# Eighty stores of a convolution and attention kernel issued from ScalarE's queue instead of SyncE's

## The chip, the cores and the metric

The kernel runs on one core of a Trainium2 chip. A core has five engines that work at once, each through its own list of instructions in order: TensorE (PE in the profile, with its weight loads as PEld), VectorE (DVE), ScalarE (ACT), GpSimd (POOL) and SyncE (SP), which only waits and issues DMAs. They meet at semaphores. The metric is the device time in microseconds of one execution, as the median of several; shorter is better. Times inside an execution are read from its profile and count from the start of the span.

## What is computed

Two independent halves are concatenated along the last axis. `A` is a long convolution whose kernel comes from a diagonal state space, `B` is attention with a learned feature map and no softmax over positions. L = S = 2048, D = 576, 128 states, 32 heads of 18.

```python
def _A_ref(u, log_A_real, A_imag, C_real, C_imag, log_dt, D_skip):
    dt = jnp.exp(log_dt)
    A = -jnp.exp(log_A_real) + 1j * A_imag
    C = (C_real + 1j * C_imag) * dt[:, None]
    P = jnp.exp((A * dt[:, None])[:, :, None] * pos[None, None, :])
    K = 2.0 * jnp.einsum("dn,dnl->dl", C, P).real
    y = irfft(rfft(u_t, 2 * L) * rfft(K, 2 * L), 2 * L)[:, :, :L]
    return y.T + u * D_skip
def _B_ref(x, wqkv, w_phi, wo):
    q, k, v = heads of x @ wqkv
    phi_q = concat(softmax(q @ w_phi), softmax(-(q @ w_phi)))      # and phi_k from k
    num = phi_q @ (phi_k^T v);  den = phi_q @ sum(phi_k) + 1e-6
    return (num / den).reshape(B, S, D) @ wo
return jnp.concatenate([a, b], axis=-1)
```

## The kernel before, in words

Everything is one program of 2902 operations. `Plan` (L171 on in the file) collects them: `op(engine, cost, function, r=..., w=...)` notes which buffers an operation reads and writes. Nothing is scheduled when the kernel is built: the table `ORDER` lists the operations by number in the order in which `Plan.run` emits them, with the buffer slot that each new tile takes and, after a `+`, how many filler matmuls go ahead of it; a `*` takes an operation's second engine. Within the table each engine's instructions keep their order, so the table sets all five queues at once. The costs written beside the operations were for the making of the table; `run` does not look at them. A DMA is an operation of engine `"sp"` whose function calls `sp.dma_start`, so it is emitted at its place in the table and is issued by SyncE in that order. It waits on SyncE's queue until its tile has been written, and the DMAs behind it in the table wait with it.

`B` runs as 16 key tiles of 128 positions (`key_tile`), the state `kv`, and 16 query tiles (`query_tile`). A query tile multiplies by the folded weight `wqT`, makes two softmaxes (q1, q2), transposes the features into `fT` (q3), multiplies by `kvb` and divides into `o` (q4), transposes `o` into `x9` (q5), multiplies by `wo` (q6), copies two halves of 288 columns from PSUM into `ot` on ScalarE or VectorE, and stores `ot`, 128 rows of 2304 bytes, into the right half of the output (L739).

`A` is a Fourier transform in stages, with tensors in DRAM between them. `u_first` transforms the input into `ud` (store at L769). `params`, `phases`, `waves` and `group` make the convolution kernel, 36 groups in 18 pairs: `waves` runs `Abs` (L909) and four sines (L916, L917) on ScalarE; `group` runs three exponentials of a PSUM tile on ScalarE (L933, L940), products on VectorE and GpSimd (L944, L948, L950 and L462), and the 64 matmuls `ps<-E,cs`. `k_first` transforms the result into `kd` (store at L983). `product` does two halves of 288 channels times eight blocks: it loads the constants `ff`, two `ub` from `ud` (L1032) and two `kb` from `kd` (L1051), multiplies, and brings the result back in `zo`, two tiles that ScalarE or VectorE copies from PSUM; both are stored into `zd[half]` (L1097), 128 rows of two runs of 1152 bytes each. `last` runs sixteen times: it loads `zi` from `zd[half]` (L1107), multiplies, copies one PSUM tile into `yo` on ScalarE or VectorE, adds and subtracts on VectorE (L466), and stores `yo` in two halves of 64 rows into the left half of the output (L1122).

The stages are not one after the other: `ORDER` mixes operations of both halves on all engines. The three kinds of store named above, 16 at L739, 32 at L1097 and 32 at L1122, lie between 252.6 and 536.5 us of the span. The PSUM tiles `ps` are 8 in all; `zo`, `ot`, `yo`, `ub`, `kb`, `fT` and others share 19 slots of one pool. L452 is the copy helper (on ScalarE and on VectorE), L455 its ScalarE form with another output type, L447 the matmul helper, L462 and L466 the tensor-tensor helper; a line of the profile with one of these stands for many places, and the tile's name tells which.

Of the kernel before, what the change touches and what calls it, by code (L numbers as in the profile page):

```python
# [170 lines left out]
class Plan:  # L171
# [24 lines left out]
    def op(self, eng, cost, fn, r=(), w=(), with_=(), table=None, busy=1.0, lock=False, mode=(128, 128), add=None):  # L196
        deps = set()
        for b in r:
            deps.update(b.writers)
        for b in w:  # L200
            deps.update(b.readers)
        if eng == "pe":
            deps.update(self.zero.writers, self.data.writers)
        k = len(self.ops)
        eng, alt = eng if isinstance(eng, tuple) else (eng, None)
        cost, alt = cost if alt is None else cost[0], alt and (alt, cost[1])
        for b in r:
            b.readers.append(k)
        for b in w:
            b.writers.append(k)  # L210
        bufs = list({id(b): b for b in (*r, *w, *with_) if not isinstance(b, Mark)}.values())
        for b in bufs:
            b.left += 1
        fill = [b for b in w if b.tag == "ps" and b.writers == [k] and not b.readers] if eng == "pe" else []
        fill = [add] if add else fill
        self.ops.append([eng, cost, fn, deps, bufs, alt, table, busy, lock, (self.unit, self.part), mode, fill[0] if fill else None, add])
# [50 lines left out]
def c_dma(nbytes, run=4096):  # L267
    return nbytes / run * (0.35 + 0.0029 * run)
# [158 lines left out]
def body(tc, nc, i, out, ctx):  # L427
    pl = Plan()
    pe, dve, act, pool, sp = nc.tensor, nc.vector, nc.scalar, nc.gpsimd, nc.sync
# [14 lines left out]
    B, op = pl.buf, pl.op  # L444

    def mm(o, l, r, start=True, stop=True, skip=False):
        pe.matmul(o, l, r, start=start, stop=stop, skip_group_check=skip)  # L447
# [102 lines left out]
    def load_again(t):  # L550
        x9 = B("x9", [128, 9, 128], F32R)
        op("sp", c_dma(128 * 4608), lambda: sp.dma_start(flat9(x9), xd[t].t), r=[xd[t]], w=[x9])
        return x9
# [15 lines left out]
    def gemm_halves(x, w, done, c0):  # L569
        r = []  # L570
        for cs, need in zip(halves, done):
            ps = B("ps", [128, 288])
            gemm(x, w, need, ps, lambda ps=ps: ps.t, slice(c0 + cs.start, c0 + cs.stop))
            r.append(ps)
        return r
# [105 lines left out]
    def query_tile(t):  # L681
        pl.at("query", t)
        ps = gemm_halves(load_again(t), wqo, (have_q[0:3], have_q[2:5]), 0)
        pl.step("q1")
        e = softmax([(ps[c], slice(16 * c, 16 * c + 16), lambda c=c: ps[c].t.rearrange("p (h f) -> p h f", f=DH)) for c in range(2)], True)
        pl.step("q3")
        fT = []
        rows = lambda j: 18 * GRP[j // 2]

        def turn(j0, n):  # L690
            tp, m, f4 = B("ps", [126, 4, 128]), rows(j0), B("fT", [126, 4, 128])
            fT.append(f4)

            def f():
                for j in range(j0, j0 + n):
                    g, sign = divmod(j, 2)
                    pe.transpose(tp.t[0:m, j - j0, :], e.t[:, sign, 7 * g:7 * g + GRP[g], :].rearrange("p h f -> p (h f)"), ident.t)  # L697
            op("pe", 110 * n, f, r=[e, ident], w=[tp], with_=[f4], busy=0.5)
            copy("any", lambda: f4.t[0:m, 0:n, :], lambda: tp.t[0:m, 0:n], [tp], [f4], 128 * n)
        for j0, n in ((0, 4), (4, 4), (8, 2)):  # L700
            turn(j0, n)
        pl.step("q4")
        o = B("o", [128, H, DH])

        def divide(g0, g1, h0, n):
            pn, den = B("ps", [128, 21, 19]), B("small", [128, 21])

            def f():
                for g in range(g0, g1):
                    hs, m = slice(7 * g, 7 * g + GRP[g]), rows(2 * g)  # L710
                    for sign in range(2):
                        j = 2 * g + sign
                        mm(pn.t[:, hs.start - h0:hs.stop - h0], fT[j // 4].t[0:m, j % 4, :], kvb.t[0:m, sign, 0:GRP[g], g, :], sign == 0, sign == 1)
            op("pe", 448 * (g1 - g0), f, r=[*fT[g0 // 2:(2 * g1 - 1) // 4 + 1], kvb], w=[pn], busy=0.4)
            op("dve", 80 + 6.7 * n, lambda: dve.reciprocal(den.t[:, :n], pn.t[:, :n, 18]), r=[pn], w=[den])
            tt("dve", lambda: o.t[:, h0:h0 + n], lambda: pn.t[:, :n, 0:18], lambda: den.t[:, :n, None].to_broadcast([128, n, DH]),
               ALU.mult, [pn, den], [o], 18 * n)
        divide(0, 3, 0, 21)
        divide(3, 5, 21, 11)
        pl.step("q5")  # L720
        tp, tq = B("ps", [128, 4, 128]), B("ps", [128, 128])
        of = lambda c: o.t.rearrange("p h f -> p (h f)")[:, c:c + 128]

        def f():
            for k in range(4):
                pe.transpose(tp.t[:, k], of(128 * k), ident.t)  # L726
            pe.transpose(tq.t, of(448), ident.t)
        op("pe", 550, f, r=[o, ident], w=[tp, tq], busy=0.5)
        o9 = B("x9", [128, 9, 128], F32R)
        copy("act", lambda: o9.t[:, 0:4], lambda: tp.t, [tp], [o9], 512)  # L730
        tt("dve", lambda: o9.t[:, 5:9], lambda: tp.t, lambda: o9.t[:, 0:4].bitcast(F32), ALU.subtract, [tp, o9], [o9], 512)
        copy("act", lambda: o9.t[64:128, 4], lambda: tq.t[64:128], [tq], [o9], 260)
        tt("dve", lambda: o9.t[0:64, 4], lambda: tq.t[64:128], lambda: o9.t[64:128, 4].bitcast(F32), ALU.subtract, [tq, o9], [o9], 245)
        pl.step("q6")
        po = gemm_halves(o9, wqo, (have_o[0:2], have_o[1:3]), D)
        ot = B("ot", [128, D])
        for c, cs in enumerate(halves):
            copy("any", lambda c=c, cs=cs: ot.t[:, cs], lambda c=c: po[c].t, [po[c]], [ot], 288)
        op("sp", c_dma(128 * 2304, 2304), lambda: sp.dma_start(out[t * 128:t * 128 + 128, 576:1152], ot.t), r=[ot])  # L739

    for t in range(NT):
        query_tile(t)
# [3 lines left out]
    kd, zd = ([B("dram", [64, 64, HD]) for _ in range(2)] for _ in range(2))  # L746
# [249 lines left out]
    par = [None] * NB  # L996
# [21 lines left out]
    def product(p, half):  # L1018
# [11 lines left out]
        four = lambda z, par: z.t[32 * par + 4 * p:32 * par + 4 * p + 4].rearrange("(j r) s d -> (r s) j d", r=2)  # L1030
# [50 lines left out]
        pz, zo = [B("ps", [128, HD]) for _ in range(4)], [B("zo", [128, 2, HD]) for _ in range(2)]  # L1081
# [10 lines left out]
        for c in range(4):  # L1092
            j, par = divmod(c, 2)
            copy("any", lambda c=c, j=j, par=par: zo[par].t[:, j], lambda c=c: pz[c].t, [pz[c]], [zo[par]], HD)

        for par in range(2):
            op("sp", c_dma(128 * 2304, 1152), lambda par=par: sp.dma_start(four(zd[half], par), zo[par].t), r=[zo[par]], w=[zd[half]])  # L1097

    for half in range(2):
        for p in range(8):  # L1100
            product(p, half)


    def last(i0, half):
        pl.at("last", 8 * half + i0 // 2)
        yo, zi = B("yo", [128, 2, HD]), B("zi", [128, 2, 2, HD])
        op("sp", c_dma(128 * 4608, 2304), lambda: sp.dma_start(  # L1107
            zi.t, zd[half].t.rearrange("q (r z b) d -> (q r) z b d", r=2, z=2)[:, :, i0:i0 + 2]), r=[zd[half]], w=[zi])
        ps = [B("ps", [128, HD]) for _ in range(2)]
        pl.step("l1")  # L1110

        def f():
            for z in range(2):
                for n in range(2):
                    mm(ps[z].t[64 * n:64 * n + 64], w3.t[:, 64 * z:64 * z + 64], zi.t[:, z, n], True, True, True)
        op("pe", 970, f, r=[zi, w3], w=ps, with_=[yo], mode=(128, 64))
        copy("any", lambda: yo.t[:, 1], lambda: ps[1].t, [ps[1]], [yo], HD)
        for z, alu in enumerate((ALU.add, ALU.subtract)):
            tt("dve", lambda z=z: yo.t[:, z], lambda: ps[0].t, lambda: yo.t[:, 1], alu, [ps[0], yo], [yo], HD)
        for n in range(2):  # L1120
            st = out.ap[0][0]
            op("sp", c_dma(64 * 2304, 1152), lambda n=n: sp.dma_start(bass.AP(  # L1122
                tensor=out.tensor, offset=out.offset + (i0 + n) * st + HD * half, ap=[[32 * st, 64], [(31 - 2 * (i0 + n)) * st, 2], [1, HD]]),
                yo.t[64 * n:64 * n + 64]), r=[yo])

    for half in range(2):
        for i0 in range(0, 16, 2):
            last(i0, half)
# [22 lines left out]
```

## Time and profile before

| | |
|---|---|
| Median of 3 runs | 540.35 us (539.47 to 544.67) |
| Profiled execution: its own time, its span | 542.0 us, 540.2 us |
| Granted TensorE clock, mean | 0.987 |
| DMA packets, bytes | 77495, 116.41 MB |
| Mean DMA rate over the span | 215 GB/s |

The profile is of one execution. Its span runs from the first to the last instruction; its own time is 1.8 us longer than the span. Busy time of an engine is time in which an instruction of it was running; waiting, semaphore instructions and the issuing of DMAs do not count as busy. In a row of a view, `out<-in` are tiles by the program's names without buffer numbers, and `SPq` is SyncE's own queue.

### The profile page before, as it was taken

The numbers are of one execution on the slowest core, as the hardware profiler recorded it, in microseconds if no ns is written. First come the engines' busy times: TensorE is split into PE (matmuls) and PEld (weight loads), VectorE is DVE, ScalarE is ACT, GpSimd is POOL, SyncE is SP. The second block draws the span as 40 slices with busy tenths as digits, with TensorE's granted clock in tenths as the row PEclk, the third lists the DMA queues.
The fourth block names the chain that finished last, engine by engine and source line by source line (L and its number), as shares of the span: only waits on it lengthen the run. The fifth ranks groups of instructions, "written<-read, shape, count | busy, mean of one in ns | idle before, by whom it ended". The sixth has DMA issues, their size and how long they took to land.

```text
span 540.2 us, 19689 instructions
## 1 busy us (share of the span) xinstructions
PE 519.9 (96%) x8186; PEld 437.3 (81%) x8186; DVE 449.5 (83%) x994; ACT 413.8 (77%) x730; POOL 331.0 (61%) x375
## 2 busy tenths in 40 slices
PE   6899999999999988999999999999999999999996
PEld 5799998999988767798887767866788887767985
DVE  3799988999999986998988989997986769878463
ACT  2699998999869977989899689799687454564442
POOL 0376798988987975975675579678454354340400
PEclk8999999999999998999999999998999999999999
DMA  8697975923317695573487956696567777997786
GB/s 227 191 358 232 350 229 202 292 80 97 119 45 234 155 324 160 139 234 109 140 225 263 303 158 199 196 277 232 176 194 233 237 216 221 289 340 241 263 265 177
DMA packets 77495, 116.41 MB, mean 215 GB/s; under 512 B 9186, under 2 KB 54370, under 8 KB 77406
## 3 DMA queue, kind: packets, MB, share of 16 engines
q1 hardware_dynamic: 77406, 115.16, 67.9%
q8 instruction: 64, 1.05, 0.8%
q14 instruction: 25, 0.20, 0.1%
HBM read 65.87 MB, written 49.26 MB: 213 GB/s over the span
## 4 chain that ended last, share of the span: by engine, by line
PE 76%; ACT 10%; DVE 6%; DMA 3%; issue 3%; POOL 1%; SPq 0%; DVEq 0%; POOLq 0%; ACTq 0%
PE ps L447 71%; PE ps L697 3%; ACT ps L933 1%; PE ps L726 1%; DMA e<-in_wkT_dram 1%; ACT zi L452 1%; ACT cs L916 1%; ACT cs L917 1%; DMA ff<-in_ff_dram 1%; ACT e L592 1%; DVE cs L944 1%; DMA dram<-zi 1%; ACT cs L909 1%; DVE E L466 1%; DVE wl L514 1%
## 5 line engine op out<-in xcount | busy, mean ns | idle before, releaser
L447 PE MATMUL ps<-wh,x 128*128 128x288 f32 (+2 forms) x1008 | 241.3, 319 | 1.9 <-ACT wh L513 1.4
L447 PEld LDWEIGHTS ps<-wh,x 128*128 128x128 f32 x1008 | 174.3, 189 | 12.8 <-ACT wh L513 1.7
L447 PE MATMUL ps<-wl,x 128*128 128x288 f32 (+2 forms) x560 | 175.9, 315 | 0.4 <-DVE wl L514 0.4
L447 PEld LDWEIGHTS ps<-wl,x 128*128 128x128 f32 x560 | 106.1, 189 | 1.7 <-DVE wl L514 0.7
L899 POOL TENSOR_TENSOR cs<-cs,pi 128x64 int32<-128x64 int32 (+4 forms) x90 | 91.5, 1017 | 6.1
L462 POOL TENSOR_TENSOR E<-v,cs 128x512 f32<-128x512 f32 x30 | 38.5, 1303 | 32.7 <-ACT v L940 31.3
L595 POOL TENSOR_TENSOR o<-e 128x576 f32<-128x576 f32 x32 | 43.1, 1346 | 18.9 <-ACT e L592 16.3
L466 DVE TENSOR_TENSOR ac<-us,ps 128x576 f32<-128x576 f32 x64 | 45.2, 744 | 6.6 <-PE ps L447 5.8
L462 POOL TENSOR_TENSOR e<-e,small 128x576 f32<-128x576 f32 x30 | 36.2, 1208 | 19.6 <-DVE small L462 13.7
L944 DVE TENSOR_TENSOR cs<-ps,cs 128x1024 f32<-128x1024 f32 x36 | 43.7, 1215 | 4.8 <-ACT ps L933 4.7
L447 PEld LDWEIGHTS ps<-E,cs 128*32 128x32 f32 x2304 | 34.6, 110 | 14.3 <-issue 10.3
L447 PEld LDWEIGHTS ps<-kvb,fT 126*128 126x128 f32 (+1 forms) x320 | 39.7, 192 | 7.7 <-issue 1.8
L462 POOL TENSOR_TENSOR e<-small,e 128x576 f32<-128x576 f32 x29 | 34.0, 1172 | 19.4 <-DVE small L462 7.9
L933 ACT ACTIVATE ps<-ps 128x512 f32<-128x512 f32 x72 | 41.6, 588 | 4.4 <-PE ps L447 3.8
L447 PE MATMUL ps<-E,cs 128*32 128x64 f32 x2304 | 40.7, 221 | 4.1 <-issue 3.5
L592 ACT ACTIVATE e<-e 128x1152 f32<-128x1152 f32 x32 | 37.3, 1167 | 8.7 <-POOL e L462 8.7
L447 PE MATMUL ps<-kvb,fT 126*128 126x133 f32 (+1 forms) x320 | 42.9, 284 | 0.6 <-DVE ac L466 0.6
L447 PE MATMUL ps<-sel,mg 128*128 128x512 f32 x108 | 41.5, 443 | 1.4 <-DVE cs L944 0.6
L452 ACT ACTIVATE zi<-ps 128x288 f32<-128x288 f32 x95 | 33.6, 413 | 9.7 <-PE ps L447 9.3
L917 ACT ACTIVATE cs<-cs,hp 128x1024 f32<-128x1024 f32 x36 | 40.6, 1141 | 0.0
L909 ACT ACTIVATE cs<-cs 128x2048 f32<-128x2048 int32 x18 | 34.4, 1913 | 5.8 <-POOL cs L899 5.6
L916 ACT ACTIVATE cs<-cs 128x1024 f32<-128x1024 int32 x36 | 36.7, 1051 | 0.2
(145 smaller groups left out, 1047.4 us busy)
## 6 DMA issues: line engine op xcount, KB each, us to landing
xd<-x SPq DMA_DIRECT2D x16, 576.0 KB
dram<-zi SPq DMA_DIRECT2D x32, 288.0 KB
dram<-zi SPq DMA_DIRECT2D x16, 576.0 KB
x<-xd SPq DMA_DIRECT2D x16, 576.0 KB
kb<-dram SPq DMA_DIRECT2D x32, 288.0 KB
ub<-dram SPq DMA_DIRECT2D x32, 288.0 KB
dram<-zo SPq DMA_DIRECT2D x32, 288.0 KB
zi<-dram SPq DMA_DIRECT2D x16, 576.0 KB
```

Source lines behind the costliest of these rows:

```text
L447: pe.matmul(o, l, r, start=start, stop=stop, skip_group_check=skip)
L452: op(("act", "dve"), (c_act(n), c_dve(n)), lambda e: act.activation(dst(), src(), AF.Copy) if e == "act" else dve.tensor_copy(dst(), src() ...
L462: op(eng, [c_dve(n[0]) if e == "dve" else c_pool(n[1]) for e in eng], lambda e: (dve if e == "dve" else pool).tensor_tensor(dst(), a(), b( ...
L466: op(eng, c_dve(n) if eng == "dve" else c_pool(n), lambda: e.tensor_tensor(dst(), a(), b(), op=alu), r=r, w=w, with_=with_, lock=eng == "p ...
L592: op("act", c_act(1152) + 40, lambda: act.activation(e.t, e.t, AF.Exp), r=[e], w=[e], table="exp")
L595: op("pool", c_pool(517), lambda: pool.tensor_tensor(pair.t, e.t[:, :, :, 0:9], e.t[:, :, :, 9:18], op=ALU.add), r=[e], w=[pair], lock=True)
L899: op("pool", c_add(4 * n * W), lambda n=n, j=j: pool.tensor_tensor(x()[:, :, :, n:2 * n], x()[:, :, :, 0:n], pi.t[:, j:j + 2, gs].bitcast( ...
L909: op(("act", "dve"), (c_act(n) + 45, c_dve(n)), lambda e: act.activation(cs.t[:, 0], x(), AF.Abs) if e == "act" else dve.scalar_tensor_ten ...
L916: op("act", c_act(64 * W) + 150, lambda at=at: act.activation(at(1), at(1).bitcast(I32), AF.Sin, scale=TURN), r=[cs], w=[sine], with_=[cs] ...
L917: op("act", c_act(64 * W) + 225, lambda at=at: act.activation(at(0), at(0), AF.Sin, scale=-TURN, bias=hp.t), r=[cs, hp, sine], w=[both], w ...
L933: op("act", c_act(512) + 12, lambda: act.activation(ps.t, ps.t, AF.Exp), r=[ps], w=[ps], table="exp")
L944: op("dve", c_dve(64 * W), lambda: dve.tensor_tensor(F(), both(M.t), F(), op=ALU.mult), r=[M, ready], w=[long], with_=[cs])
```

## The change

The three stores call `act.dma_start` in place of `sp.dma_start`; `act` is `nc.scalar`, `sp` is `nc.sync`. Nothing else differs: the operations keep engine `"sp"` and their cost in the plan, and the order table is the same. The 80 DMAs stand at the same places in the table, and there they now belong to ScalarE's list of instructions, between the ScalarE operation that the table has before them and the one after. The other 283 DMAs stay with SyncE.

```diff
@@ query_tile
-        op("sp", c_dma(128 * 2304, 2304), lambda: sp.dma_start(out[t * 128:t * 128 + 128, 576:1152], ot.t), r=[ot])
+        op("sp", c_dma(128 * 2304, 2304), lambda: act.dma_start(out[t * 128:t * 128 + 128, 576:1152], ot.t), r=[ot])
@@ product
-            op("sp", c_dma(128 * 2304, 1152), lambda par=par: sp.dma_start(four(zd[half], par), zo[par].t), r=[zo[par]], w=[zd[half]])
+            op("sp", c_dma(128 * 2304, 1152), lambda par=par: act.dma_start(four(zd[half], par), zo[par].t), r=[zo[par]], w=[zd[half]])
@@ last
-            op("sp", c_dma(64 * 2304, 1152), lambda n=n: sp.dma_start(bass.AP(
+            op("sp", c_dma(64 * 2304, 1152), lambda n=n: act.dma_start(bass.AP(
                 tensor=out.tensor, offset=out.offset + (i0 + n) * st + HD * half, ap=[[32 * st, 64], [(31 - 2 * (i0 + n)) * st, 2], [1, HD]]),
                 yo.t[64 * n:64 * n + 64]), r=[yo])
```

## The prediction, made before the change was run

> **What bounds the kernel now.** I read the page's busy times first, then a table of stretches around the stores, then the chain that ended last, and then who waits for whom. The page:
>
> ```profile
> PE 519.9 (96%) x8186; PEld 437.3 (81%) x8186; DVE 449.5 (83%) x994; ACT 413.8 (77%) x730; POOL 331.0 (61%) x375
> ```
>
> The table of stretches (us, then busy time and count of PE, PEld, DVE, ACT, POOL, then clock, DMA share, GB/s), from just ahead of the first store to the end of the last matmul:
>
> ```profile
> 252.00:340.00 88.00, 85.98 (x1547) 68.33 (x1549) 78.67 (x176) 76.19 (x136) 59.26 (x68) 1.00 0.68 207
> 340.00:420.00 80.00, 78.17 (x1486) 60.74 (x1479) 66.36 (x143) 65.65 (x104) 47.66 (x47) 0.98 0.72 227
> 420.00:500.00 80.00, 79.99 (x1266) 62.07 (x1277) 63.83 (x144) 41.02 (x105) 28.34 (x30) 1.00 0.81 255
> 500.00:536.50 36.50, 36.06 (x311) 31.42 (x279) 18.78 (x48) 15.44 (x36) 7.53 (x7) 1.00 0.78 240
> ```
>
> TensorE is the bound: from 252 us to its last matmul it lacks 2.02 + 1.83 + 0.01 + 0.44 = 4.3 us of being always busy. ScalarE has room on the whole, but unevenly: 11.8 us idle of 88, then 14.4 of 80, then 39.0 of 80. What TensorE waits for from 252 us on (the chain of waits of that stretch; total, times, longest):
>
> ```profile
> PE ps L447 <- DMA ff<-in_ff_dram: 0.4, 1, 0.4
> ...
> PEld ps L447 <- ACT zo L452: 2.5, 6, 0.5
> PEld ps L447 <- ACT us L452: 2.5, 6, 0.5
> ...
> PEld ps L447 <- DMA ub<-dram: 0.5, 1, 0.5
> ```
>
> Loads delay it by 0.4 + 0.5 us in all. Its weight loads wait for ScalarE's PSUM copies at a dozen places already: there a later copy has nothing to hide behind.
>
> **What is removed.** SyncE's queue waits for the data of the stores, with the loads of the table behind them:
>
> ```profile
> SPq L1097 <- ACT zo L452: 19.4, 8, 5.9
> SPq L739 <- ACT ot L452: 15.7, 8, 4.5
> ...
> SPq L1122 <- DVE yo L466: 11.8, 7, 4.1
> ```
>
> The largest row of each comes to 46.9 us of SyncE's waiting together, and up to 5.9 us at once. Loads behind them can leave earlier. What that is worth is what TensorE waits for loads, 0.9 us at most: the loads are early enough as they are. I count −0.9.
>
> The Trainium skill, page "Perfetto Trace Analysis", section "DMA Optimizations", suggests one DMA-capable engine for inputs and another for outputs, to let them move more freely. That is this change; by that rule it is a gain, a rival below. The trace agrees that stores hold up loads on SyncE, and not that the loads are late.
>
> **What is added: issue time on ScalarE.** A DMA issue on SyncE lasts (min/median/max, ns):
>
> ```profile
> L739 SPq DMA_DIRECT2D out_dram<-ot x16: 337/354/1266, 252.6 to 536.5; - x16
> L1097 SPq DMA_DIRECT2D dram<-zo x32: 359/421/1402, 298.8 to 502.2; - x32
> L1122 SPq DMA_DIRECT2D out_dram<-yo x32: 595/604/1324, 410.1 to 534.8; - x32
> ```
>
> No DMA of ScalarE's stands in the trace; I take SyncE's medians, with the same rows' maxima as the upper end and nothing (hidden under a running activation) as the lower. 16 x 0.354 + 32 x 0.421 + 32 x 0.604 = 38.5 us. ScalarE has 65 us idle from 252 to 500 us, so the sum would fit; but it takes its list in order, so a store that is not ready holds what is behind it. The cost is therefore read place by place. By the order table I know which ScalarE instruction stands behind each store.
>
> The Trainium skill, page "DMA: Bandwidth & Descriptors", section "Issuing engines are not separate DMA queues", says that issuing from several engines saves only the sequencer's time of issue, usually small beside the transfer. By it the bytes move no faster (the sum goes without a gain in bandwidth); it says nothing of what waits behind an issue.
>
> *Place 1, 381 us, the worst.* The second `zo` store of product 1 stands ahead of the four sines at 376.85, but VectorE copies its tile only at 380.69:
>
> ```profile
> 376.85 2.01 ACT L916 ACTIVATE cs<-cs 128x1024 f32<-128x1024 int32 x2
> 378.76 2.18 ACT L917 ACTIVATE cs<-cs,hp 128x1024 f32<-128x1024 f32 x2
> 380.95 1.28 ACT L933 ACT_TABLE_LOAD   x1
> 383.83 0.58 ACT L933 ACTIVATE ps<-ps 128x512 f32<-128x512 f32 x1 [1.60 <-PE ps L447]
> 385.19 0.60 ACT L940 ACTIVATE v<-ps 128x512 f32<-128x512 f32 x1 [0.77 <-DMA dram<-zo]
> ...
> 387.01 0.71 ACT L452 ACTIVATE zo<-ps 128x288 f32<-128x288 f32 x2 [0.92 <-PE ps L447]
> 387.64 0.58 ACT L933 ACTIVATE ps<-ps 128x512 f32<-128x512 f32 x1
> ```
>
> ```profile
> 380.69 0.43 DVE L452 COPY zo<-ps 128x288 f32<-128x288 f32 x1
> ...
> 388.25 1.22 DVE L944 TENSOR_TENSOR cs<-ps,cs 128x1024 f32<-128x1024 f32 x1
> ```
>
> ```profile
> 389.62 1.10 PE L447 MATMUL ps<-E,cs 128*32 128x64 f32 x64
> ```
>
> The tile is ready at 381.12, the issue ends at 381.6, the sines start there, 4.7 us late. They last 4.1 us (376.85 to 380.94), to 385.7; the table load 1.28, to 387.0; so the exponential of 383.83 starts at 387.0, 3.1 us late. Two idle gaps ahead of 387.01, 0.77 and 0.92, take back 1.7: 1.4 is left; query 9's `ot` store, between the two copies of 387.01, adds 0.35. The exponential of 387.64 is 1.8 us late, and VectorE's product of 388.25 (ends 389.47) and the matmuls of 389.62 stand right behind it. TensorE loses 1.8 us. This hangs on the wait, not on the price of an issue.
>
> *Place 2, 521 us.* Two `yo` stores of `last` 15 stand between the two `fT` copies of query 14; they left SyncE at 520.98, when the tile was ready:
>
> ```profile
> 520.40 1.08 ACT L452 ACTIVATE fT<-ps 126x512 f32<-126x512 f32 x2 [2.16 <-PE ps L697]
> ```
>
> ```profile
> 520.98 1.90 SPq L1122 DMA_DIRECT2D out_dram<-yo  x3
> ```
>
> ```profile
> 521.57 4.16 PE ps L447 x34
> ```
>
> The second copy ends at 521.48, and the chain that ended last goes on with matmuls at 521.57. Behind two issues of 0.60 it starts at 522.28 in place of 520.89: 1.4 us.
>
> *Place 3, 410 us.* The first `yo` store of `last` 1 stands ahead of ScalarE's small copy:
>
> ```profile
> 408.95 0.27 ACT L452 ACTIVATE ks<-ps 128x128 f32<-128x128 f32 x1
> ```
>
> ```profile
> 409.66 0.45 DVE L466 TENSOR_TENSOR yo<-ps,yo 128x288 f32<-128x288 f32 x1
> ```
>
> ```profile
> 411.87 2.53 POOL L462 TENSOR_TENSOR E<-v,cs 128x512 f32<-128x512 f32 x2 [12.74 <-ACT v L940]
> ```
>
> ```profile
> 415.22 1.10 PE L447 MATMUL ps<-E,cs 128*32 128x64 f32 x64
> ```
>
> The tile is ready at 410.11, the copy starts at 410.8, 1.8 us late, the exponentials behind the table load about 1.7. GpSimd's products, begun at 411.87, end at 414.40, and the matmuls need them at 415.22: 0.8 is free. 0.9 us.
>
> *The tail.* Matmuls end just ahead of the last copy into `ot`; its store is the last thing issued:
>
> ```profile
> 534.31 0.71 ACT L452 ACTIVATE ot<-ps 128x288 f32<-128x288 f32 x2 [3.55 <-PE ps L447]
> 536.09 0.41 ACT L452 ACTIVATE ot<-ps 128x288 f32<-128x288 f32 x1 [1.07 <-PE ps L447]
> ```
>
> Seven of the last `yo` stores, 4.2 us, stand ahead of the copies of 534.31, in a gap of 3.55 us: those copies are a microsecond late, the last one, behind query 14's store, about 0.4.
>
> *The rest, an estimate.* Of the dozen waits of TensorE's weight loads above, the six on `zo` stand among the `zo` stores themselves: 6 x 0.42 = 2.5. Of the six on `us` I take half as standing behind a store: 3 x 0.42 = 1.3. Bounds for the rest: nothing, and all the other issue time, some 34 us.
>
> *Sum:* 1.8 + 1.4 + 0.9 + 0.4 + 2.5 + 1.3 − 0.9 = 7.4 us. The profiled execution had a span of 540.2 and a time of 542.0; the median of the runs shown is 540.35. I add to the median: **547.8 us**, +1.4%, in the range of its own case 546 to 556.
>
> **The rivals.**
>
> *It is hidden.* The issues run under activations, and delays of a microsecond end in waits that later work has anyway. For it: 39 us idle on ScalarE from 420 to 500, where most `yo` and `zo` stores stand. Against it: TensorE has only 4.3 us of gaps to swallow anything in. Left are place 1 and the tail, 2.2, less 0.9: 541.7 us. Up to 545.7 I count it as no change.
>
> *Faster: the loads run free.* If loads that leave up to 5.9 us earlier empty the buffers' queue ahead of TensorE, its gaps from 252 to 500 us close: 3.86 us, to 536.5; it is faster by over 1% only if the stretched matmuls inside the busy time shorten as well by 1.6 us or more. That decides where TensorE's gaps end with a load; the trace shows 0.9 us of such. Time: 534.
>
> *ScalarE becomes the bound.* If an issue there costs more than on SyncE (the rows go to 1.3 and 1.4 us), or each delay reaches VectorE, whose late tiles then hold the next store, ScalarE is full from 252 to 420, where it has 26 us idle. Half of the 38.5 us reaching the end gives 560.
>
> *It does not do what it says:* the issues stay tied to SyncE's progress, should a DMA of ScalarE's have to wait until earlier ones of SyncE's have landed. That takes away the 0.9 and nothing else: 548.7, in the forecast's case.
>
> **How the numbers follow.** A measurement of this kernel can tell about 1%, 5.4 us, from no change. Forecast, 546 to 556: 0.57; ScalarE the bound, above 556: 0.07; hidden: 0.30; loads free: 0.06. So slower 0.64, same 0.30, faster 0.06. The range takes in most of the hidden case, which begins near 541.7: 541.5 to 556.
>
> **What would show it.** The profile after should have a second hardware DMA queue beside SyncE's, issues of 0.35 to 0.6 us at ScalarE's queue, and ScalarE's sines of group 16 waiting for VectorE's `zo` at what is now 376.85, with a gap of TensorE near 389 of 1 to 2 us and another near 521. TensorE's busy share falls to about 95%, since its work is the same. SyncE's waits on L739, L1097 and L1122 vanish, and TensorE's waits for loads stay under 1 us. Wrong it would be if TensorE's gaps did not grow, or if its busy time itself fell.

## The result and the profile after

The changed kernel took 557.92 us (median of 4 executions, 551.85 to 559.01), the kernel before beside it 542.14 us (4, 539.47 to 544.67): a ratio of 1.0253 (95% interval 1.0208 to 1.0298), slower, about 13.7 us. The ratio, here and below, is taken over undisturbed executions alone, so it is not the quotient of the two medians. The profiled execution took 557.3 us with a span of 555.5, 15.3 us longer than the span of before. Two parts of its page, the busy times and the hardware DMA queues (packets, MB, share of 16 engines):

```profile
PE 525.3 (95%) x8186; PEld 436.2 (79%) x8186; DVE 452.1 (81%) x994; ACT 414.3 (75%) x730; POOL 330.0 (59%) x375
...
q1 hardware_dynamic: 61790, 96.28, 55.2%
q10 hardware_dynamic: 15616, 18.88, 10.7%
```

A second hardware queue, q10, carries the stores. The counts of instructions are those of before. TensorE's share falls from 96 to 95%; 5.4 us of the added time lies inside its busy time (519.9 before), as stretched matmuls. The table of stretches, in the columns used in the prediction:

```profile
252.00:340.00 88.00, 84.79 (x1509) 66.13 (x1511) 75.94 (x169) 74.77 (x132) 56.33 (x64) 1.00 0.68 204
340.00:420.00 80.00, 76.82 (x1451) 58.48 (x1439) 64.28 (x138) 64.18 (x103) 46.01 (x47) 1.00 0.70 222
420.00:500.00 80.00, 75.38 (x1134) 57.81 (x1142) 58.71 (x133) 39.55 (x98) 31.98 (x33) 1.00 0.76 233
500.00:552.00 52.00, 48.90 (x526) 40.25 (x495) 29.64 (x71) 20.18 (x49) 8.34 (x8) 1.00 0.68 218
```

TensorE's idle time is 3.21 + 3.18 + 4.62 + 3.10 = 14.1 us where it was 4.3. The third stretch, with 0.01 us idle before, has the largest part of it, and fewer matmuls fit in (1134, not 1266), although ScalarE is busy for only half of it. The clock column is the same in it (1.00); from 340 to 420 us it is 1.00 where it was 0.98. The issues at ScalarE's queue:

```profile
L739 ACTq DMA_DIRECT2D out_dram<-ot x16: 338/357/439, 252.7 to 552.3; - x16
L1097 ACTq DMA_DIRECT2D dram<-zo x32: 366/367/594, 299.9 to 515.1; - x32
L1122 ACTq DMA_DIRECT2D out_dram<-yo x32: 602/603/2039, 414.2 to 550.1; - x32
```

The medians are close to SyncE's (354, 421 and 604 before). The 80 add up to 5.8 + 12.9 + 22.1 = 40.8 us of ScalarE's queue; 13.0 us of that lie under a running activation. From the end of ScalarE's instruction ahead to the moment the tile was ready, it also stood waiting in front of them for 0.0 + 4.1 + 4.7 = 8.8 us. What TensorE waits for from 252 us on (us, times, longest):

```profile
PEld ps L447 <- ACT fT L452: 4.7, 4, 1.8
...
PEld ps L447 <- ACT v L940: 2.9, 4, 1.7
...
PEld ps L447 <- ACT us L452: 2.8, 7, 0.6
PEld ps L447 <- ACT zo L452: 2.6, 6, 0.6
...
PEld ps L447 <- DVE ks L466: 2.2, 2, 2.0
...
PE ps L447 <- ACT fT L452: 2.1, 2, 1.6
...
PEld ps L447 <- DMA kb<-dram: 1.2, 1, 1.2
...
PE ps L447 <- DMA ub<-dram: 1.1, 1, 1.1
...
PE ps L447 <- DMA ff<-in_ff_dram: 0.8, 1, 0.8
...
PE ps L447 <- DMA kb<-dram: 0.7, 1, 0.7
```

The waits for `zo` and `us`, which the prediction multiplied by an issue time, have hardly grown. What has grown are the waits for ScalarE's copies of `fT` (0.6 us before), for its exponentials `v` (none before) and for the small tile `ks` (0.2 before from VectorE). And the loads, which were to come earlier, come later: 3.8 us of waiting in the last four rows (the two of `kb` in part the same time), 4.3 with one more row of 0.5, where it was 0.9. SyncE's own queue shows why they could not run free; first before, then after:

```profile
SPq L1032 <- DMA dram<-zo: 5.5, 3, 3.3
...
SPq L1107 <- DMA dram<-zo: 3.9, 3, 1.9
```

```profile
SPq L1107 <- DMA dram<-zo: 25.6, 4, 16.1
...
SPq L1032 <- DMA dram<-zo: 19.0, 5, 7.7
```

SyncE no longer waits at L739, L1097 and L1122 for data, but its loads now wait longer until the `zo` stores have landed, 44.6 us in these two rows where it was 9.4: the wait has moved by one step. That this is what makes TensorE wait for loads is not shown: "short, no wait" in the experiments below leaves all stores on SyncE, and there TensorE waits 3.8 us for loads, with 10.4 us in the same two rows of SyncE.

**Where the time went.** TensorE runs the same 8186 matmuls in the same order in both traces, so the start of each can be set against its start before. The difference grows by this much in each stretch (time of before, us), for the change and for the experiments below, by whose names the rows go. Differences ahead of 252 us, where no store stands, drop out; they go from −3.1 us ("long, wait") to +6.7 us ("the other 50"), so a row need not add up to its kernel's ratio:

| | 252–340 | 340–372 | 372–386 | 386–400 | 400–420 | 420–436 | 436–458 | 458–492 | 492–520 | 520–537 |
|---|---|---|---|---|---|---|---|---|---|---|
| the change | +3.04 | +0.07 | −1.77 | +2.73 | +1.76 | +2.00 | −0.01 | +3.96 | +1.54 | +1.83 |
| only `ot` | +2.21 | +0.01 | −2.38 | +0.18 | 0.00 | 0.00 | −0.01 | +0.95 | −0.02 | 0.00 |
| only `zo` | +1.47 | +0.06 | −2.09 | +2.73 | +0.01 | 0.00 | 0.00 | +0.49 | +1.56 | +0.34 |
| only `yo` | −1.76 | 0.00 | −2.44 | 0.00 | +1.77 | +0.61 | 0.00 | +1.22 | −0.01 | +0.81 |
| the 30 | +1.70 | +0.07 | −1.81 | +2.77 | +1.74 | +0.97 | 0.00 | +1.30 | +1.56 | +0.77 |
| the other 50 | −0.33 | +0.01 | −2.09 | −0.01 | +0.01 | +0.01 | 0.00 | +1.79 | −0.01 | 0.00 |
| short, no wait | +1.82 | −0.01 | −1.75 | +0.33 | 0.00 | 0.00 | 0.00 | +2.10 | +0.13 | 0.00 |
| short, wait | +0.98 | +0.01 | −2.11 | +1.79 | +1.25 | +0.01 | 0.00 | +1.06 | +0.56 | +0.17 |
| long, no wait | +1.77 | +0.29 | −1.81 | +1.03 | +0.43 | +0.57 | 0.00 | +0.49 | +0.82 | +0.57 |
| long, wait | +3.76 | +0.39 | −2.47 | +2.85 | +1.87 | +1.75 | 0.00 | +2.53 | +1.34 | +1.18 |
| moved to gaps | −0.90 | −0.01 | −2.08 | +0.75 | +0.01 | +0.01 | 0.00 | +3.11 | +1.85 | 0.00 |
| the same, second session | −1.82 | 0.00 | −2.03 | +0.50 | +0.02 | 0.00 | −0.01 | +2.48 | +0.97 | 0.00 |
| the same, 23 back | −1.32 | −0.02 | −2.08 | +0.33 | +0.02 | +0.39 | 0.00 | +2.33 | −0.02 | 0.00 |

The first row adds up to 15.15 us. The −1.8 to −2.5 at 372 to 386 us stand in every row, also where no store was moved ("short, no wait"): that is a loss in the one profiled execution of before, not a gain of any change. Its trace shows the reason: the granted clock is 0.58 from 374 to 378 us, an estimated (1 − 0.58) x 4 = 1.7 us lost, and no other trace has a lowered clock between 320 and 535 us. Kernels with the same stores on ScalarE agree from 386 to 420 us to a few hundredths (2.73, 2.73, 2.77; 1.76, 1.77, 1.74); 252 to 340 and 458 to 492 scatter by one to two: only `yo` has no moved store ahead of 400 us and still −1.76, and "short, no wait" moves none at all and has +1.82 and +2.10 (the +2.21 of only `ot` holds a stretch of lowered clock of its own, at 315 us). There I read only differences larger than that.

### The profile page after: what moved, and what is told of

It reads as the page before. It is cut to its first block, busy times and chain, and to the rows that moved or that the text cites. A ratio compares the mean times of both kernels' runs of the same rounds, so it can differ in the third digit from the quotient of the medians.

```text
span 555.5 us, 19666 instructions
## 1 busy us (share of the span) xinstructions
PE 525.3 (95%) x8186; PEld 436.2 (79%) x8186; DVE 452.1 (81%) x994; ACT 414.3 (75%) x730; POOL 330.0 (59%) x375
## 4 chain that ended last, share of the span: by engine, by line
PE 57%; ACT 13%; DVE 11%; DMA 5%; POOL 5%; issue 4%; ACTq 2%; SPq 0%; POOLq 0%; DVEq 0%
PE ps L447 54%; POOL cs L899 2%; PE ps L697 2%; DVE cs L944 2%; ACTq L1122 2%; ACT ps L933 1%; DVE yo L466 1%; ACT cs L909 1%; POOL e L462 1%; DMA kb<-dram 1%; ACT zi L452 1%; ACT e L592 1%; DMA out_dram<-yo 1%; ACT cs L916 1%; DMA ff<-in_ff_dram 1%
## 5 line engine op out<-in xcount | busy, mean ns | idle before, releaser
L462 POOL TENSOR_TENSOR E<-v,cs 128x512 f32<-128x512 f32 x30 | 38.6, 1306 | 40.7 <-ACT v L940 40.6
L592 ACT ACTIVATE e<-e 128x1152 f32<-128x1152 f32 x32 | 37.3, 1167 | 10.5 <-POOL e L462 10.4
```

The source lines that it names most:

```text
L462: op(eng, [c_dve(n[0]) if e == "dve" else c_pool(n[1]) for e in eng], lambda e: (dve if e == "dve" else pool).tensor_tensor(dst(), a(), b( ...
L592: op("act", c_act(1152) + 40, lambda: act.activation(e.t, e.t, AF.Exp), r=[e], w=[e], table="exp")
```

## Experiments

Three theories. **Theory 1, the place:** ScalarE takes its list in order; a store that stands ahead of work which TensorE is about to need holds that work for the wait and the issue, and only such places cost. **Theory 2, the time:** each issue costs its share of the 40.8 us on ScalarE, wherever it stands. **Theory 3, the coupling:** a store in a second queue and the loads in the first wait for each other's completions, so that the number of stores counts. Ratios are to the kernel before, run in the same session (medians 542.3 to 544.1 us), with 95% intervals; in us they are given at 542. Each diff shows the part of a line that changes; where it shows one kind of store, the other two change likewise.

**One kind of store at a time.** Each is one of the three edits of the change, here `ot`:

```diff
-lambda: sp.dma_start(out[t * 128:t * 128 + 128, 576:1152], ot.t)
+lambda: act.dma_start(out[t * 128:t * 128 + 128, 576:1152], ot.t)
```

> Only the 16 ot stores on ScalarE. Theory 1, places: what counts is which ScalarE work stands behind a store that is not ready or is being issued; from the steps in which the matmuls of the changed kernel fall behind those of before (0.8 us at 253, 0.4 at 287, some 0.5 at 387), 2 us slower. Theory 2, issue time: every issue costs a fixed share of its length, 15.8 of 37 us = 0.43; 16 x 0.357 x 0.43 = 2.4 us. Theory 3, coupling of the two queues: a store on ScalarE and a load on SyncE wait for each other's earlier transfers whatever their number, so that a large part of the 15.8 us, over 5, is there already.

> Only the 32 zo stores on ScalarE. Theory 1, places: the steps at 303, 315, 330, 387 to 390, 461, 480, 494 and 508 us add to 7 to 8 us slower. Theory 2, issue time: 32 x 0.367 x 0.43 = 5.1 us. Theory 3, coupling: over 5 us, and with the same number of DMAs as only_yo about the same as that one.

> Only the 32 yo stores on ScalarE. Theory 1, places: the steps at 414 to 417, 425 and 522 us add to about 5 us slower. Theory 2, issue time: 32 x 0.603 x 0.43 = 8.3 us, the largest of the three. Theory 3, coupling: as only_zo.

Measured: `ot` 544.37 us, 0.9985 (0.9943 to 1.0028); `zo` 550.53 us, 1.0147 (1.0091 to 1.0204), +8.0 us; `yo` 545.99 us, 1.0044 (1.0008 to 1.0081), +2.4 us. The `yo` stores take most of the issue time, 22.1 of 40.8 us, and cost less than a third of `zo`: Theory 2 in its plain form falls, and Theory 3, by which two sets of 32 cost alike, with it. Theory 1 has the order right, but `yo` came out at half of what I expected and `ot` at nothing. The three sum to about 10 us of 13.7, which their intervals, 2 to 3 us each, leave room for; that some places need two kinds at once is not shown. At 420 to 436 us only-`yo` loses 0.61 of the change's 2.00, and at 520 to 537 it loses 0.81 of 1.83: in the change's profile one issue at each of these two places took 2.04 and 1.62 us, in only-`yo` none over 1.10.

**The 30 stores at the bad places, and the other 50.** From the two traces I took the stores next to which the change's matmuls fell behind: 5 `ot`, 17 `zo`, 8 `yo`.

```diff
+HELD = {"ot": {2, 15, 12, 9, 5}, "zo": {(3, 0), (3, 1), ...}, "yo": {1, 5, 3, 15}}
-lambda par=par: sp.dma_start(four(zd[half], par), zo[par].t)
+lambda par=par: (act if (8 * half + p, par) in HELD["zo"] else sp).dma_start(four(zd[half], par), zo[par].t)
```

> 30 of the 80 stores on ScalarE: those that stand where the changed kernel's matmuls fell behind (5 ot, 17 zo, 8 yo); the other 50 on SyncE. Theory 1, places: nearly all of the loss, 11 to 15 us slower. Theory 2, issue time: 12.8 us of issue x 0.43 = 5.5 us. Theory 3, coupling: between, by number 30 of 80, 6 us, or nearly all.

> Only the other 50 of the 80 stores go out on ScalarE's queue; the 30 at places where the matmuls of the changed kernel fell behind stay on SyncE. Theory 1 (what costs is the place: ScalarE, in order, is held at a store in front of work that TensorE is about to need): these 50 are nearly free, ratio to before 0.997 to 1.008 (-1.5 to +4 us). Theory 2 (each issue costs its own time on ScalarE, wherever it stands): 50 of 80 stores, 50/80 of 13.8 = +8.6 us, ratio 1.016. Theory 3 (each store in ScalarE's queue also waits for the eighth DMA before it, in either queue, and the loads wait for it in turn, so that the number of stores counts): +6 us or more, ratio above 1.011.

Measured: the 30 553.96 us, 1.0175 (1.0096 to 1.0254), +9.5 us; the other 50 543.35 us, 0.9983 (0.9945 to 1.0021), −0.9 us. Theory 2 gave the 50 +8.6, Theory 3 +6 or more; both lie outside the interval. The 30 came out below the 11 to 15 us that Theory 1 gave them, and their interval, 5.2 to 13.8 us, alone would not exclude the 5.5 of Theory 2; the 50 decide. The table agrees: the 50 lose 0.01 us at most in each of the stretches from 386 to 436 and nothing from 492 on, where the 30 lose 5.5 and 2.3. So do the traces: of the 14.1 us of issues of the 30, 2.4 lie under a running activation, of the 26.6 us of the 50, 10.2. What a store costs depends on where it stands.

**All 80 on ScalarE, 43 of them later in the table.** Each store goes to the first gap of ScalarE, in the profile of before, in which its tile is ready and its issue fits. The table changes by such moves, here the second `zo` store of product 1, operation 2446, which now follows ScalarE's four sines:

```diff
-... 2417 2444* 2446 2355/0 2301 609/6 2561* 2414 930*/6 2299
+... 2417 2444* 2355/0 2301 609/6 2561* 2414 930*/6 2299 ...
...
-... 2361/3 929/5 2300 2562* 2563* 561* 2362 2356* ...
+... 2361/3 929/5 2300 2562* 2563* 561* 2446 2362 2356* ...
```

> All 80 stores on ScalarE's queue as in the change, but 43 of them stand later in the order table: each at the first gap of ScalarE in the profile of before in which its tile is ready and its issue (0.36, 0.37 or 0.60 us) ends before ScalarE's next work begins. Nothing is taken from the work or from the number of issues. Theory 1 (place): most of the loss goes, ratio to before 0.993 to 1.010, and well below the changed kernel's 1.025. Theory 2 (issue time wherever it stands): about as slow as the change, ratio 1.020 to 1.026. Theory 3 (the queues are coupled through the order of all DMAs): as the change or slower, since the stores come later in that order.

> The run with all 80 stores on ScalarE and 43 of them moved to its gaps, once more beside the run with 57, for a tighter interval: ratio to before 1.000 to 1.007, and above the run with 57 if the late loads are what is left.

Measured: 546.90 us, 1.0036 (0.9998 to 1.0074), and in a second session 546.87 us, 1.0094 (1.0057 to 1.0132). The second lies above the 1.000 to 1.007 that I expected of it. Both are well below the change's 1.0253, with the same 80 issues on the same queue: Theory 2 is out, and 63 to 86% of the loss is gone by order alone. Of the 40.6 us of issues in the first session's trace 21.8 lie under running activations, 13.0 of 40.8 in the change's. At place 1 ScalarE's timeline of this kernel reads:

```profile
377.50 2.01 ACT L916 ACTIVATE cs<-cs 128x1024 f32<-128x1024 int32 x2
379.41 1.14 ACT L917 ACTIVATE cs<-cs,hp 128x1024 f32<-128x1024 f32 x1
379.95 0.37 ACTq L1097 DMA_DIRECT2D dram<-zo  x1
380.45 1.14 ACT L917 ACTIVATE cs<-cs,hp 128x1024 f32<-128x1024 f32 x1
```

The store stands behind the last of the four sines in the table; no sine waits for it, and the issue lies wholly under the third one. The places at 400 to 436 and 520 us lose 0.01 us or nothing. It is still no faster than before: what is left stands mostly in the stretches from 458 to 520 us.

**Is the rest of it late loads?** The same kernel with the 23 stores of 458 to 506 us back on SyncE at their old places:

```diff
-lambda par=par: act.dma_start(four(zd[half], par), zo[par].t)
+lambda par=par: (sp if half else act).dma_start(four(zd[half], par), zo[par].t)
```

> As the run with 43 stores moved to gaps of ScalarE, but the 23 stores that SyncE issued between 458 and 506 us before (the sixteen of products 8 to 15, attention outputs 3, 5 and 6, last 2 and 3) are back on SyncE, at their places in the table of before; 57 stores stay on ScalarE. In that stretch TensorE waited for loads in the run with all 80 moved. If those loads were late because the stores sit on the other queue, that stretch gives back its 5 us: from 458 to 520 us the matmuls lose no more than 1.5 us, TensorE's waits for loads from 470 us on fall from 3.1 us to about 1, and the ratio to before is 0.994 to 1.002. If what is left has another cause, the stretch loses 3 us or more as it did, ratio 1.002 to 1.007.

Measured: median 545.08 us, 1.0030 (0.9998 to 1.0063). The ratio alone decides nothing: it lies in the range of the second expectation, its interval reaches into the first, and it is below the 1.0094 (1.0057 to 1.0132) of all 80 in the same session, as late loads would have it. The stretch from 458 to 520 us lies between the two, with +2.3 us, neither under 1.5 nor over 3. Its waits for loads from 470 us on are these rows:

```profile
PE ps L447 <- DMA ub<-dram: 0.7, 1, 0.7
PE ps L447 <- DMA kb<-dram: 0.7, 1, 0.7
...
PEld ps L447 <- DMA kb<-dram: 0.5, 1, 0.5
```

Together they are 1.9 us, above the 1 that was expected if late loads were the cause, and below both profiles with all stores on ScalarE (4.4 us in the first session, 2.6 in the second, summed over the rows of `ub` and `kb`). Those two are the same kernel, and differ by 1.8 us, more than the 0.7 us between the 57 and all 80 in one session; so this one is inconclusive. 492 to 520 us lost nothing here, and 1.85 and 0.97 in the two profiles with all 80; only `zo` loses 1.56 there, only `ot` and only `yo` nothing: that part belongs to the `zo` stores of this stretch.

**The wait and the time apart.** Here the stores stay on SyncE. At each store's place ScalarE runs activations of two elements per partition, 0.20 us each; what they write is used by nothing. They read the tile to be stored (wait) or the identity matrix (no wait); one each (short, 16 us in all) or two and three (long, about the time of the issues).

```diff
-lambda: sp.dma_start(out[t * 128:t * 128 + 128, 576:1152], ot.t)
+lambda: (act.activation(hp.t[:, 1:3], ot.t[:, 0:576:575], AF.Copy), sp.dma_start(out[t * 128:t * 128 + 128, 576:1152], ot.t))[1]
```

That is the short one with the wait. The tile `hp` gets two more columns for it; its first column keeps the constant that the sines use.

> The stores stay on SyncE. At each store's place in the table ScalarE runs an activation of two elements per partition that reads the tile to be stored (its result is used by nothing), so that ScalarE waits there for the tile as in the change, but issues no DMA. Theory 1 (place, head of the line): more than half of the 13.8 us, ratio to before 1.012 to 1.025, and clearly above the same activations without the wait. Theory 2 (issue time): the activations take about 0.2 us where an issue takes 0.36 to 0.60, so about half the loss, and as much with a tile that is long there. Theory 3 (queue coupling): no more than +3 us, ratio below 1.006.

> As the run with the small activations, but each of the 80 reads two columns of the identity matrix, written at the start, so that ScalarE spends the same time and waits for no tile. Theory 1 (place, head of the line): 0 to +4 us, ratio to before 1.000 to 1.007. Theory 2 (issue time): about +6 us, ratio 1.011, and the same as with the wait. Theory 3 (queue coupling): 0 to +3 us.

> Stores on SyncE. In front of each store ScalarE runs as many of the two-element activations that read the tile as make up about the time of the change's issue: two for an attention or convolution store (0.41 us beside 0.36 and 0.37), three for one of the last stage (0.61 beside 0.60). So ScalarE waits for the tile and is held as long as in the change, and no DMA is issued from it. Theory 1 (place and length of the stay at the head of the line): nearly all of the change's loss, ratio to before 1.018 to 1.026. Theory 3 (the rest of the loss is a coupling of the two DMA queues or the long issues of up to 2.04 us): no more than the run with one activation, ratio 1.008 to 1.014.

> The same two and three activations per store as the run before it, reading the identity matrix, so without the wait: 80 pieces of 0.41 to 0.61 us of ScalarE's time, 39 us in all, close to the 40.8 us that the 80 issues of the change take on ScalarE. Theory 1 (what costs is the tile that is late, and the time only adds behind it): ratio to before 1.002 to 1.008. Theory 2 (time on ScalarE costs wherever it stands): 1.015 to 1.025, about as the change.

The added activations of the long run with the wait:

```profile
L739 ACT ACTIVATE hp<-ot x32: 190/205/228, 249.7 to 547.6; 128x2 f32<-128x2 f32 x32
L1097 ACT ACTIVATE hp<-zo x64: 190/205/226, 296.6 to 510.9; 128x2 f32<-128x2 f32 x64
L1122 ACT ACTIVATE hp<-yo x96: 191/203/219, 411.6 to 545.8; 64x2 f32<-64x2 f32 x96
```

32 x 0.205 + 64 x 0.205 + 96 x 0.203 = 39.2 us, against 40.8 us of issues.

| | no wait | wait |
|---|---|---|
| short | 544.39 us, 1.0012 (0.9981 to 1.0043) | 550.48 us, 1.0109 (1.0045 to 1.0173) |
| long | 548.72 us, 1.0134 (1.0051 to 1.0218) | 555.83 us, 1.0241 (1.0172 to 1.0311) |
| the change | | 557.92 us, 1.0253 (1.0208 to 1.0298) |

The last two rows answer Theory 3: with no DMA on ScalarE at all, only the wait and the time in its list, the loss is 1.0241, indistinguishable from the change's 1.0253. No coupling of the queues is needed for the total, though the intervals leave room for some 4 us either way. The stand-in is not exact: 13.0 us of the change's issues lay under running activations, and an added activation takes its 0.20 us of the engine itself (ScalarE's busy time goes from 413.8 to 447.4 us), so it may cost more than the issue that it stands for, and a coupling of some size could hide in the difference. Against one speak two things. In the long run with the wait SyncE waits only 8.1 us for the landing of `zo` stores, against 44.6 in the change, and TensorE still waits 3.0 us for loads. And in the trace of the change none of the 80 issues starts more than 0.44 us after both its tile was ready and the instruction ahead of it had begun, or, if that is an issue, had ended. The wait adds about 1.0% in both rows, the longer stay 1.2 to 1.3% in both columns. The short run with the wait came out just under the 1.012 that Theory 1 gave it. Here I was half wrong: I expected the long run without the wait at 1.002 to 1.008, and it came out at 1.0134. Time alone at these places costs too, and not in proportion: the first 16 us next to nothing, the next 23 us some 6.6. Together with the run moved to gaps the reading is that the place matters for both: in a gap an issue is nearly free, in front of urgent work it is paid for.

## Why the prediction was wrong

The direction was right, the mechanism too, and the three named places did cost; the size was not: 547.8 us forecast, range to 556.0, median 557.92. By its own steps:

*Place 1, 381 us: 1.8 predicted, 2.3 measured.* The timeline of the changed kernel, all engines, and then TensorE's:

```profile
382.27 0.43 DVE L452 COPY zo<-ps 128x288 f32<-128x288 f32 x1
...
382.73 0.37 ACTq L1097 DMA_DIRECT2D dram<-zo  x1
...
383.14 2.01 ACT L916 ACTIVATE cs<-cs 128x1024 f32<-128x1024 int32 x2 [1.60 <-DVE us L452]
```

```profile
389.68 0.50 PE L447 MATMUL ps<-sel,mg 128*128 128x512 f32 x1 [1.13 <-ACT v L940]
...
393.25 1.10 PE L447 MATMUL ps<-E,cs 128*32 128x64 f32 x64
```

By the table the kernel was 1.38 us behind here. The sines start at 383.14 in place of 376.85, 4.9 us late beyond that (predicted 4.7). The issue follows the end of VectorE's copy by 0.03 us, as foreseen, though the row names the `us` copy beside it as the releaser. The matmuls of 389.62 start at 393.25: 3.63 − 1.38 = 2.25 us. The way was not quite the one foretold: these matmuls wait for nothing here, TensorE lost 1.2 us ahead of them, at a matmul that needs the exponential `v` (389.68, before 387.11), and the rest at the `kb` matmuls after it, which wait for copies of `fT` and `zo`. All are ScalarE's work behind the sines. Only `zo` alone loses the same in this stretch, +2.73 of +2.73, and the run with the sines in front of the store 0.75.

*Place 2, 521 us: 1.4 predicted, 1.8 measured.*

```profile
534.45 2.27 ACTq L1122 DMA_DIRECT2D out_dram<-yo  x2
536.76 0.60 ACT L452 ACTIVATE fT<-ps 126x512 f32<-126x512 f32 x1 [2.40 <-DMA out_dram<-yo]
```

```profile
537.41 1.59 PE L447 MATMUL ps<-kvb,fT 126*128 126x133 f32 x12 [1.56 <-ACT fT L452]
```

The two issues took 2.27 us where I had put two of 0.60. The second `fT` copy stands behind them, TensorE behind the copy. That the two figures are so near is luck: the 1.07 us above my two issues come from one long one, and where the issues are shorter the place costs less than forecast, 0.81 us in only `yo` and 0.77 in the 30.

*Place 3, 410 us: 0.9 predicted, 1.8 measured.*

```profile
414.25 0.70 ACTq L1122 DMA_DIRECT2D out_dram<-yo  x1
415.00 0.28 ACT L452 ACTIVATE ks<-ps 128x128 f32<-128x128 f32 x1 [1.83 <-DVE yo L466]
```

```profile
417.75 2.51 POOL L462 TENSOR_TENSOR E<-v,cs 128x512 f32<-128x512 f32 x2 [14.43 <-ACT v L940]
```

The kernel was 4.11 us behind. The copy is 1.9 us late beyond that (predicted 1.8) and GpSimd's products 1.8 (1.7): the chain was right, and so was it that 0.8 us of it is free: 56 of the 64 matmuls that use GpSimd's products are 0.85 us late beyond the 4.11. The rest came by a second way that the prediction did not follow:

```profile
420.32 0.99 PE L447 MATMUL ps<-E,cs 128*32 128x64 f32 x56 [0.16 <-POOL E L462]
421.24 0.73 PE L447 MATMUL ps<-sel,mg 128*128 128x512 f32 x2
422.33 0.50 PE L447 MATMUL ps<-sel,mg 128*128 128x512 f32 x1 [0.36 <-DVE e L466]
```

VectorE waits for the same exponential (its product of 411.22 starts at 417.27), so it too is 1.9 us late, and its later work `e` on a PSUM tile holds the last of the next matmuls, which brings the loss to 1.8.

*The tail: 0.4 predicted, 0.1 measured* (15.3 us of span less 15.2 at the last matmul). Seven `yo` issues do hold the first of the last copies, but TensorE goes on meanwhile.

```profile
546.04 4.64 ACTq L1122 DMA_DIRECT2D out_dram<-yo  x7
550.73 0.71 ACT L452 ACTIVATE ot<-ps 128x288 f32<-128x288 f32 x2 [4.30 <-DMA out_dram<-yo]
```

*The loads freed: −0.9 predicted, no gain.* The rows above have TensorE waiting for loads 4.3 us in place of 0.9, though as much was seen with no store moved. The prediction took it that SyncE without stores is SyncE ahead of time; its loads need slots and data which the `zo` stores release.

*The rest: 3.8 predicted, about 10 measured.* **This is the step that failed.** In the table it is +3.04 at 252 to 340 us, +2.00 at 420 to 436, +3.96 at 458 to 492, +1.54 at 492 to 520, in all 10.5. The first and third of these scatter by one to two us, and the third has part of the late loads, so 10.5 is this profile's figure; the 30 give 5.5 in the same four. By the ratio, 13.7 us less the 5.8 of the three places leaves about 7.9 for the rest, the tail and the loads, where 3.8 + 0.4 − 0.9 = 3.3 were forecast. The estimate multiplied an issue time by nine waits that were there already, for `zo` and `us`. The waits that came were at other tiles, `fT`, `v`, `ks` and the loads. The clearest is one that I could have found as I found place 2: the two `yo` stores of `last` 5 stand ahead of a small copy `ks`, which before ended 1.65 us ahead of the matmuls that need it:

```profile
423.26 0.28 ACT L452 ACTIVATE ks<-ps 128x128 f32<-128x128 f32 x1 [0.52 <-PE ps L447]
```

```profile
425.19 1.01 PE L447 MATMUL ps<-ks,w 32*128 32x288 f32 x12
```

and after, ScalarE's and TensorE's timeline:

```profile
428.84 2.68 ACTq L1122 DMA_DIRECT2D out_dram<-yo  x2
431.57 0.28 ACT L452 ACTIVATE ks<-ps 128x128 f32<-128x128 f32 x1 [2.66 <-PE ps L447]
```

```profile
432.89 1.50 PE L447 MATMUL ps<-ks,w 32*128 32x288 f32 x20 [1.76 <-DVE ks L466]
```

The copy is 8.31 us later, the matmuls 7.70; with 5.87 us lost before, 2.4 and 1.8 are this place's. The wait is put down to TensorE and VectorE; by the two issues in front of it, it was ScalarE's list. One of the two is the issue of 2.04 us; with none so long, only `yo` loses 0.61 in this stretch and the 30 lose 0.97. The sum of the three places, 4.1 predicted, was 5.8: too small by 1.7, and the rest by 6.7. −1.8 us of the comparison belongs mostly to the lowered clock in the profile of before, as said.

*The rivals.* "Hidden" fell for the whole: ScalarE's idle time from 420 us on does not help where a place is in front of an urgent copy. For 50 of the 80 stores it holds: alone they cost nothing that can be measured. "ScalarE the bound", 560 us with a chance of 0.07, was nearest in time, but not in cause: ScalarE's busy share, in which issues do not count, went from 77 to 75%, it is about 80% with the 27.8 us of issues that lie under no activation, and the same 80 issues in its gaps cost 0.4 to 0.9%. "It does not do what it says" fell too: the issue of place 1 left 0.03 us after its tile was ready. "Loads run free" fell: TensorE waits for loads no less than before. The Trainium skill, page "Perfetto Trace Analysis", section "DMA Optimizations", says that one engine for inputs and another for outputs may make sense, to allow more dynamic spread. No gain of that kind shows here, with 1.0253. The Trainium skill, page "DMA: Bandwidth & Descriptors", section "Issuing engines are not separate DMA queues", says that issuing on several engines saves only the sequencer's time of issue. The trace agrees in that nothing moved faster (210 GB/s over the span, 215 before), and adds that the time saved on SyncE's queue is paid on ScalarE's, in order.

What stays open: the stretch from 458 to 492 us, where loads are late by an amount that varies between executions; what part of "the rest" is that scatter; and why some issues take 2 us.

## What to carry to other kernels

Before a DMA is moved to a computing engine's queue, read for each one what stands behind it in that engine's list, when its data is ready, and how long the work behind can wait before the bound engine notices; the total of issue time against the engine's idle time did not tell it here. Go through all of them: an average price times the waits that the profile already shows misses the waits that will be new. If the queue must be used, put each issue behind the urgent work, at the first gap after its data is ready; here that took 2.5% down to 0.4 to 0.9%, and SyncE's queue, which has no computing to hold up, was still at least as good.

## What the runs showed of the hardware

A DMA issue takes on ScalarE's queue about what it takes on SyncE's (0.357, 0.367 and 0.603 us in the median, 0.354, 0.421 and 0.604 on SyncE), and it can lie under a running activation. Not expected: ScalarE's queue can issue a DMA before an activation that stands ahead of it in its list has started. In the timeline of the kernel with moved stores above, the issue of 379.95 us stands behind the sine of 380.45. So an issue whose data is ready can be cheaper than its length: in that kernel 32 of the 80 issues lay wholly under running activations, in the change 14.

Also not expected: the second of two `yo` issues in a row took 2.04 us once and 1.62 us once, where the other thirty stayed under 0.8; no row says what for. It is not ScalarE's alone: with only `ot` moved, a `yo` issue on SyncE took 2.52 us. And 192 activations of two elements, 0.20 us each, with nothing to wait for, cost 1.3% (1.0051 to 1.0218) on an engine that is busy for 77% of the time, while 80 of them cost 0.1% (0.9981 to 1.0043).
